# Batch loads into packed 192-byte rows, and weights staged in tiles of their own

## The chip, the cores and the metric

The kernel runs on one core of one Trainium2 chip. The metric is the device time of one execution in microseconds, lower is better; where there are several runs, their median.

## The reference

A gated linear attention runs over 4 batches, 8 heads, 768 steps and a head size of 48. Its output, laid side by side over the heads (3072 rows of 384), goes through a feed-forward layer that takes the larger of two projections:

```python
f = 1.0 / (1.0 + np.exp(-f_logit))
for t in range(S):
    state = f[:, :, t, :, None] * state + np.einsum('bhd,bhe->bhde', k[:, :, t], v[:, :, t])
    y[:, :, t] = np.einsum('bhd,bhde->bhe', q[:, :, t], state)

x = y.transpose(0, 2, 1, 3).reshape(B * S, H * D)
out = np.maximum(x @ w1, x @ w2) @ w_out      # w1, w2: 384 x 1024, w_out: 1024 x 384
```

All inputs and the output are float32.

## The kernel before

The 768 steps of a batch are cut into 6 chunks (`nch`) of 128 (`C`), which makes 24 chunks (`T`), numbered over the batches. In SBUF the partition is the step within the chunk.

**Loads.** For each of f, k, q and v there are two buffers (`lb`), used by even and odd batches: 128 partitions by 8 heads, 6 chunks and 64 floats (`DP`), of which 48 (`D`) are used. So every row of 48 floats, 192 bytes, begins on a multiple of 256 bytes. `load(i)` (L60) brings one chunk of all four inputs, 192 KB each; `load_batch(b, names)` (L67) brings all six chunks of a batch at once, 1.18 MB for each input. In DRAM the steps of a head lie one behind the other, so two rows that lie side by side in a partition are 128 steps apart in DRAM, and two rows in neighbouring partitions are adjacent there. All loads and all stores are issued on one queue, SyncE's (SP), in the order of the program text.

**Order of the queue.** Chunks 0 to 2, the weights w2 and w_out, chunk 3, the weight w1, chunks 4 and 5 (L81 to L88); then batch 1 (issued at the end of the loop's step 0), f and v of batch 2 (step 1), k and q of batch 2 (step 2), the stores of group 0 (steps 6 and 7), f and v of batch 3 (step 7), k and q of batch 3 (step 8), and the other stores. A store waits on the queue for its data, and all that is behind it waits too.

**Weights.** The three weight matrices have no tiles of their own: `w1_f`, `w2_f` and `wo_f` (L77 to L79) are views of the second buffers of f, k and q. They are read by `u_w2_cast` (VectorE), `u_wo_cast` (ScalarE) and `u_wd` (VectorE, `wd` = w1 - w2). The layer is computed as relu(x (w1 - w2)) w_out + x (w2 w_out), where w2 w_out is made once (`u_w2T`, `u_w2o`).

**The loop.** Each step i runs parts of several chunks: `s_y(i)` (state and output), `s_tr(i+2)` (transposes), `s_a(i+1)` (products within a chunk, masked), `s_cum(i+3)` (running sums of the gates, and scaled k and q on GpSimd), `s_xT(i)` (transpose of the result), `s_ell(i+4)` (the gate's logarithm, and v cast to bf16 on VectorE). Four chunks make a group. When a group is complete, `push_group` puts 16 units of the feed-forward layer into a list: eight `u_d` (a block of d_ff, the relu into `gT`) and two halves of `u_o` for each of four output tiles; the second half copies the result to `ob` (VectorE, L186) and stores it (L188). Between the parts of a step one unit each is taken from the list, four in a step, so a group's output copies fall into two steps out of four, two copies in each. Every engine works through its instructions in this order. The group's last units run after the loop.

The work tiles that the change touches have these numbers of buffers before: `gT` 2, `ob` 3, `e` 2, `tmp` 2, `xT` 3.

Of the kernel before, what the change touches and what calls it, by code (L numbers as in the profile page):

```python
# [11 lines left out]
F32 = mybir.dt.float32  # L12
BF16 = mybir.dt.bfloat16
# [4 lines left out]
def kernel(  # L18
# [15 lines left out]
    B, H, S, D = q.shape  # L34
    C = 128
    nch = S // C
    dm = H * D
    d_ff = moe_w1.shape[1]
    JG = dm // C
    FG = d_ff // C  # L40
    DP = 64
    NP = H // 2
    T = nch * B
    GT = B * C

    ctx.enter_context(tc.manual_schedule())
    consts = ctx.enter_context(tc.tile_pool(name="consts", bufs=1))
    work = ctx.enter_context(tc.tile_pool(name="work", bufs=2))
# [6 lines left out]

    SRC = (("f", f_logit), ("k", k), ("q", q), ("v", v))

    lb = {n: [consts.tile([C, H, nch, DP], F32, name=f"{n}b{x}") for x in range(2)] for n, _ in SRC}

    def load(i):  # L60
        b, c = divmod(i, nch)
# [11 lines left out]
    def loaded(i, name):  # L73
        b, c = divmod(i, nch)
        return lb[name][b % 2][:, :, c, 0:D]

    w1_f = lb["f"][1].rearrange("p h c d -> p (h c d)").rearrange("p (j f) -> p j f", j=JG)  # L77
    w2_f = lb["k"][1].rearrange("p h c d -> p (h c d)").rearrange("p (j f) -> p j f", j=JG)
    wo_f = lb["q"][1].rearrange("p h c d -> p (h c d)").rearrange("p (j f) -> p j f", j=FG)  # L79

    for i in range(3):  # L81
        load(i)
# [74 lines left out]
    xT_g = {}  # L157

    def push_group(g):
        gT = work.tile([C, FG, GT], BF16, name="gT", tag="gT")  # L160
        xT = xT_g[g]

        def u_d(f):
            ps = ps_m.tile([C, GT], F32, name="d", tag="mm")
            for j in range(JG):
                nc.tensor.matmul(out=ps, lhsT=wd[:, j, f * C:(f + 1) * C], rhs=xT[:, j, :],  # L166
                                 start=(j == 0), stop=(j == JG - 1))
            nc.scalar.activation(gT[:, f, :], ps, AF.Relu)  # L168

        hold = {}  # L170

        def u_o(b, half):
            ts = slice(b * C, (b + 1) * C)
            if half == 0:
                hold[b] = ps_m.tile([C, dm], F32, name="o", tag="mm")
            ps = hold[b]
            mms = [(xT[:, j, ts], w2o[:, j, :]) for j in range(JG)]
            mms += [(gT[:, f, ts], wo[:, f, :]) for f in range(FG)]
            cut = 6
            todo = range(0, cut) if half == 0 else range(cut, len(mms))  # L180
            for n in todo:
                nc.tensor.matmul(out=ps, lhsT=mms[n][0], rhs=mms[n][1],  # L182
                                 start=(n == 0), stop=(n == len(mms) - 1))
            if half == 1:
                ob = work.tile([C, dm], F32, name="ob", tag="ob", bufs=3)
                nc.vector.tensor_copy(ob, ps)  # L186
                r0 = (g * B + b) * C
                nc.sync.dma_start(out=out[r0:r0 + C, :], in_=ob)  # L188

        for f in range(FG):  # L190
            units.append(lambda f=f: u_d(f))
        for b in range(B):
            units.append(lambda b=b: u_o(b, 0))
            units.append(lambda b=b: u_o(b, 1))
# [9 lines left out]
    def s_ell(i):  # L204
        b, c = divmod(i, nch)
        t = {n: loaded(i, n) for n in "fkqv"}
        e = work.tile([C, dm], F32, name="e", tag="e")
        ell = ell_b[i % 2]
        nc.scalar.activation(e.rearrange("p (h d) -> p h d", h=H), t["f"], AF.Exp, scale=-1.0)  # L209
        nc.scalar.activation(ell[:, :, 0:D], e.rearrange("p (h d) -> p h d", h=H), AF.Ln, bias=1.0)  # L210
        vb = work.tile([C, dm], BF16, name="vb", tag="vb", bufs=6)
        nc.vector.tensor_copy(vb.rearrange("p (h d) -> p h d", h=H), t["v"])  # L212
        st[i] = {"ell": ell, "v": vb}
# [50 lines left out]
    def s_y(i):  # L264
        b, c = divmod(i, nch)
        s = st[i]
        am, vb, tr = s["am"], s["v"], s["tr"]
        old, new = st_b[b][c % 2], st_b[b][(c + 1) % 2]
        if c < nch - 1:
            sa = ps_s.tile([C, NP, 2 * D], F32, name="sa", tag="s")  # L270
            for p in range(NP):
                nc.tensor.matmul(out=sa[:, p, :],  # L272
                                 lhsT=s["kp"][:, 2 * p:2 * p + 2, :].rearrange("p h d -> p (h d)"),
                                 rhs=vb[:, 2 * p * D:(2 * p + 2) * D], start=True, stop=True)
            tmp = work.tile([C, NP, 2 * D], F32, name="tmp", tag="tmp")
            nc.vector.tensor_add(tmp, sa, old)  # L276
            for o in range(2):
                r, e = slice(o * DP, (o + 1) * DP), slice(o * D, (o + 1) * D)
                nc.gpsimd.tensor_mul(new[r, :, e], tmp[r, :, e],  # L279
                                     s["fl"][r, :].unsqueeze(2).to_broadcast([DP, NP, D]))  # L280
        y = ps_s.tile([C, dm], F32, name="y", tag="s")
        for p in range(NP):
            if c > 0:
                nc.tensor.matmul(out=y[:, 2 * p * D:(2 * p + 2) * D], lhsT=tr[:, 1, p, :],  # L284
                                 rhs=old[:, p, :], start=True, stop=False)
            for o in range(2):
                h = 2 * p + o
                ds = slice(h * D, (h + 1) * D)
                nc.tensor.matmul(out=y[:, ds], lhsT=am[:, o, p, :], rhs=vb[:, ds],  # L289
                                 start=(c == 0), stop=(c == 0 or o == 1))  # L290
        x = work.tile([C, dm], BF16, name="x", tag="x")
        nc.scalar.copy(x, y)  # L292
        s["x"] = x

    def s_xT(i):
        b, c = divmod(i, nch)
        s = st.pop(i)
        g, n = divmod(i, B)
        if n == 0:
            xT_g[g] = work.tile([C, JG, GT], BF16, name="xT", tag="xT", bufs=3)  # L300
        ps = ps_s.tile([C, JG, C], BF16, name="xtp", tag="s")
        for j in range(JG):
            nc.tensor.transpose(out=ps[:, j, :], in_=s["x"][:, j * C:(j + 1) * C], identity=ident)
        nc.vector.tensor_copy(xT_g[g][:, :, n * C:(n + 1) * C], ps)  # L304


    for i in range(-4, T):
        if i >= 0:
            s_y(i)
        unit()  # L310
        if 0 <= i + 2 < T:
            s_tr(i + 2)
        unit()
        if 0 <= i + 1 < T:
            s_a(i + 1)
        unit()
        if 0 <= i + 3 < T:
            s_cum(i + 3)
        unit()
        if i >= 0:  # L320
            s_xT(i)
        if i < B:
            unit()
            unit()
        if i >= 0 and i % B == B - 1:
            push_group(i // B)
        if 0 <= i + 4 < T:
            s_ell(i + 4)
        if i == 0:
            load_batch(1, "fkqv")  # L330
        if i >= 0 and i % nch == 1 and i // nch + 2 < B:
            load_batch(i // nch + 2, "fv")
        if i >= 0 and i % nch == 2 and i // nch + 2 < B:
            load_batch(i // nch + 2, "kq")
# [32 lines left out]
```

## Time and profile before

| | |
|---|---|
| median of 2 runs | 221.16 us (220.6 and 221.72) |
| the profiled execution's own time | 222.57 us |
| its span, first to last instruction | 220.8 us |
| busy: PE / VectorE / ScalarE / GpSimd | 145.7 / 101.4 / 86.5 / 75.5 us |
| mean granted TensorE clock | 0.876 |
| DMA | 28.54 MB, 129 GB/s on average |

The profile gives the busy time of each engine and cuts the span into 40 equal slices of 5.5 us; a digit there is a tenth of the slice. "PEclk" is the granted clock of TensorE in tenths. In rows of waits stand the engine and its line, what it waited for, the total in us, the number of times and the longest. Rows of a timeline begin with the start and the duration in us, then the engine, the line, the operation, what it writes and reads, and in brackets the idle time ahead of it and what ended it. "SPq" is the DMA queue of SyncE; a duration there is the time that issuing took, not the transfer. Rows of windows give, for a stretch of time, the busy time of each engine, the granted clock, the DMA engines' share and GB/s. L64 is line 64 of the kernel.

### The profile page before, as it was taken

Reading aid. Unit: us, or ns where it says so; the run is one execution under the profiler, and the core shown is the slowest. Engines: PE = TensorE matmul, PEld = TensorE weight load, DVE = VectorE, ACT = ScalarE, POOL = GpSimd, SP = SyncE. Lnnn points to the kernel's source line nnn. Section 1 sums busy time; section 2 is a strip of 40 time slices with the busy share of each in tenths; the row PEclk is TensorE's granted clock in tenths of the full one; section 3 lists DMA queues with packets and bytes.
Section 4 is the critical chain, followed back from the end, with each engine's and each line's share of the span. In section 5 each row is a group of like instructions: output and inputs, shape, how many; then the busy total and the mean of one; then the engine's idle time right before and its main releaser. Section 6 shows DMA issues by size and latency. Waiting matters only on the chain.

```text
span 220.8 us, 3530 instructions
## 1 busy us (share of the span) xinstructions
PE 145.7 (66%) x1384; PEld 87.6 (40%) x1384; DVE 101.4 (46%) x161; ACT 86.5 (39%) x200; POOL 75.5 (34%) x107
## 2 busy tenths in 40 slices
PE   0000169468700088995699970689998999999893
PEld 0000155345500044563345640345654565456451
DVE  8002333787200165762456540466665666564122
ACT  2000463644520027644176440176457645640610
POOL 8000035376300073553145430155553555520000
PEclk9999999955555569999589995599999999999999
DMA  8999999979999999999599989200210012002012
GB/s 123 163 172 393 256 324 173 107 133 163 163 168 163 163 163 166 163 166 179 150 159 167 167 150 186 100 0 0 74 71 3 0 73 76 0 3 106 36 39 107
DMA packets 48897, 28.54 MB, mean 129 GB/s; under 512 B 25584, under 2 KB 48112, under 8 KB 48880
## 3 DMA queue, kind: packets, MB, share of 16 engines
q1 hardware_dynamic: 48880, 28.32, 71.0%
q8 instruction: 11, 0.18, 0.4%
q14 instruction: 6, 0.05, 0.1%
HBM read 23.59 MB, written 4.72 MB: 128 GB/s over the span
## 4 chain that ended last, share of the span: by engine, by line
PE 33%; issue 19%; DMA 17%; POOL 14%; SPq 10%; ACT 4%; DVE 2%; POOLq 0%; DVEq 0%; ACTq 0%
PE o L182 12%; PE d L166 11%; SPq L70 10%; DMA out_dram<-ob 9%; DMA vb<-in_v_dram 8%; POOL qp L234 6%; POOL kp L233 5%; PE tr L242 4%; PE a L257 3%; ACT ei L229 3%; POOL st L108 1%; ACT gT L168 1%; PE y L284 1%; DVE ob L186 1%; PE y L289 1%
## 5 line engine op out<-in xcount | busy, mean ns | idle before, releaser
L233 POOL TENSOR_TENSOR kp<-kb,ei 128x384 bf16<-128x384 f32 x24 | 24.9, 1039 | 84.7 <-ACT ei L229 76.4
L166 PE MATMUL d<-xT,wd 128*128 128x512 bf16 x144 | 41.6, 410 | 14.1 <-DVE xT L304 13.9
L168 ACT ACTIVATE gT<-d 128x512 bf16<-128x512 f32 x48 | 29.0, 603 | 35.5 <-PE d L166 35.1
L182 PE MATMUL o<-wo,gT 128*128 128x384 bf16 x192 | 37.7, 326 | 0.0
L279 POOL TENSOR_TENSOR st<-tmp,fl 64x192 bf16<-64x192 f32 x40 | 20.1, 503 | 36.4 <-DVE tmp L276 35.0
L260 DVE TENSOR_TENSOR am<-a,mask 128x1024 bf16<-128x1024 f32 x24 | 29.2, 1219 | 4.3 <-PE a L257 4.3
L186 DVE COPY ob<-o 128x384 f32<-128x384 f32 x24 | 13.4, 558 | 35.7 <-PE o L182 20.5
L246 DVE COPY trs<-tr 128x1024 bf16<-128x1024 bf16 x24 | 16.6, 691 | 28.7 <-PE tr L242 28.7
L234 POOL TENSOR_TENSOR qp<-qb,ed 128x384 bf16<-128x384 f32 x24 | 27.1, 1129 | 0.0
L229 ACT ACTIVATE ei<-cum 128x384 f32<-128x384 f32 x24 | 11.7, 489 | 38.0 <-PE cum L223 38.0
L212 DVE CAST vb<-vb 128x384 bf16<-128x384 f32 x24 | 15.8, 658 | 19.5 <-DMA vb<-in_v_dram 19.5
L166 PEld LDWEIGHTS <-wd 128*128 128x128 bf16 x144 | 12.4, 102 | 24.2 <-issue 16.4
L182 PEld LDWEIGHTS <-gT 128*128 128x128 bf16 x192 | 17.8, 97 | 10.4
L292 ACT CAST x<-y 128x384 bf16<-128x384 f32 x24 | 11.2, 467 | 22.2 <-PE y L289 22.1
L134 PE MATMUL w2tp<-ident,w_h 128*128 128x128 bf16 x24 | 3.5, 308 | 22.3 <-DVE w_h L122 22.3
L272 PE MATMUL sa<-vb,kp 128*128 128x96 bf16 x80 | 7.3, 220 | 16.3 <-DVE tmp L276 15.5
L182 PE MATMUL o<-w2o,xT 128*128 128x384 bf16 x72 | 15.7, 326 | 0.0
L242 PE MATMUL tr<-ident,qp 128*128 128x128 bf16 x96 | 11.3, 251 | 6.2 <-POOL qp L234 5.6
L289 PE MATMUL y<-vb,am 128*128 128x48 bf16 x192 | 12.3, 191 | 2.2 <-DVE am L260 1.7
L221 PE MATMUL cum<-ell,ut 128*128 128x384 bf16 x24 | 9.1, 378 | 6.0 <-ACT ell L210 6.0
L209 ACT ACTIVATE e<-fb 128x384 f32<-128x384 f32 x24 | 13.0, 541 | 0.0
L210 ACT ACTIVATE ell<-e 128x384 bf16<-128x384 f32 x24 | 12.6, 523 | 0.9
(42 smaller groups left out, 183.7 us busy)
## 6 DMA issues: line engine op xcount, KB each, us to landing
out_dram<-ob SPq DMA_DIRECT2D x24, 192.0 KB, 1.9
kb<-in_moe_w_dram SPq DMA_DIRECT2D x1, 1536.0 KB, 7.8
qb<-in_moe_w_out_dram SPq DMA_DIRECT2D x1, 1536.0 KB, 11.0
fb<-in_moe_w_dram SPq DMA_DIRECT2D x1, 1536.0 KB, 7.9
fb<-in_f_logit_dram SPq DMA_DIRECT2D x6, 192.0 KB, 5.3
kb<-in_k_dram SPq DMA_DIRECT2D x6, 192.0 KB, 5.4
qb<-in_q_dram SPq DMA_DIRECT2D x6, 192.0 KB, 5.4
vb<-in_v_dram SPq DMA_DIRECT2D x6, 192.0 KB, 5.0
```

Of the source, the lines that this page charges most:

```text
L70: nc.sync.dma_start(out=lb[name][b % 2][:, :, :, 0:D].rearrange("p h c d -> p (h c) d"), in_=src[b].rearrange("h (c p) d -> p (h c) d", c= ...
L166: nc.tensor.matmul(out=ps, lhsT=wd[:, j, f * C:(f + 1) * C], rhs=xT[:, j, :], start=(j == 0), stop=(j == JG - 1))
L168: nc.scalar.activation(gT[:, f, :], ps, AF.Relu)
L182: nc.tensor.matmul(out=ps, lhsT=mms[n][0], rhs=mms[n][1], start=(n == 0), stop=(n == len(mms) - 1))
L212: nc.vector.tensor_copy(vb.rearrange("p (h d) -> p h d", h=H), t["v"])
L229: nc.scalar.activation(ei, ps[:, 0:dm], AF.Exp)
L233: nc.gpsimd.tensor_mul(kp[:, :, 0:D], t["k"], ei.rearrange("p (h d) -> p h d", h=H))
L234: nc.gpsimd.tensor_mul(qp[:, :, 0:D], t["q"], ed.rearrange("p (h d) -> p h d", h=H))
L242: nc.tensor.transpose(out=ps[:, n, p, :], in_=src[:, 2 * p:2 * p + 2, :].rearrange("p h d -> p (h d)"), identity=ident)
L246: nc.vector.tensor_copy(tr, ps)
L260: nc.vector.tensor_mul(am.rearrange("p o n c -> p (o n) c"), ps.rearrange("p o n c -> p (o n) c"), mask)
L279: nc.gpsimd.tensor_mul(new[r, :, e], tmp[r, :, e], s["fl"][r, :].unsqueeze(2).to_broadcast([DP, NP, D]))
```

## The change

The load buffers get rows of 48 floats instead of 64: a partition's 48 rows of a batch then adjoin, and a row begins at a multiple of 192 bytes. The buffers shrink from 12288 to 9216 bytes a partition, and no longer have the size of a weight matrix; the three weights get tiles of their own, 12288 bytes a partition each. Five kinds of work tiles get fewer buffers. The text of `load`, `load_batch` and `loaded` stays as it is, and so do the order of the queue and of the loop.

```diff
-    lb = {n: [consts.tile([C, H, nch, DP], F32, name=f"{n}b{x}") for x in range(2)] for n, _ in SRC}
+    lb = {n: [consts.tile([C, H, nch, D], F32, name=f"{n}b{x}") for x in range(2)] for n, _ in SRC}
...
-    w1_f = lb["f"][1].rearrange("p h c d -> p (h c d)").rearrange("p (j f) -> p j f", j=JG)
-    w2_f = lb["k"][1].rearrange("p h c d -> p (h c d)").rearrange("p (j f) -> p j f", j=JG)
-    wo_f = lb["q"][1].rearrange("p h c d -> p (h c d)").rearrange("p (j f) -> p j f", j=FG)
+    w1_f = consts.tile([C, JG, d_ff], F32, name="w1_f")
+    w2_f = consts.tile([C, JG, d_ff], F32, name="w2_f")
+    wo_f = consts.tile([C, FG, dm], F32, name="wo_f")
...
-        gT = work.tile([C, FG, GT], BF16, name="gT", tag="gT")
+        gT = work.tile([C, FG, GT], BF16, name="gT", tag="gT", bufs=1)
...
-                ob = work.tile([C, dm], F32, name="ob", tag="ob", bufs=3)
+                ob = work.tile([C, dm], F32, name="ob", tag="ob", bufs=2)
...
-        e = work.tile([C, dm], F32, name="e", tag="e")
+        e = work.tile([C, dm], F32, name="e", tag="e", bufs=1)
...
-            tmp = work.tile([C, NP, 2 * D], F32, name="tmp", tag="tmp")
+            tmp = work.tile([C, NP, 2 * D], F32, name="tmp", tag="tmp", bufs=1)
...
-            xT_g[g] = work.tile([C, JG, GT], BF16, name="xT", tag="xT", bufs=3)
+            xT_g[g] = work.tile([C, JG, GT], BF16, name="xT", tag="xT", bufs=2)
```

## The prediction

> **What bounds the kernel now.** I read the page's slices first, then the table of waits, then the DMA queue's own timeline, then VectorE's timeline around the long waits. The slices are 5.5 us each.
>
> ```profile
> span 220.8 us, 3530 instructions
> PE   0000169468700088995699970689998999999893
> PEclk9999999955555569999589995599999999999999
> DMA  8999999979999999999599989200210012002012
> GB/s 123 163 172 393 256 324 173 107 133 163 163 168 163 163 163 166 163 166 179 150 159 167 167 150 186 100 0 0 74 71 3 0 73 76 0 3 106 36 39 107
> ```
>
> The DMA engines are nearly always busy up to 138 us, at about 165 GB/s, and nearly idle afterwards. PE has two holes in that time (near 65 us and 135 us) and is dense after it. So up to 138 us the loads set the pace, and after it the engines do. The waits and the queue say which loads:
>
> ```profile
> ACT wo L126 <- DMA qb<-in_moe_w_out_dram: 23.3, 1, 23.3
> DVE vb L212 <- DMA vb<-in_v_dram: 19.5, 1, 19.5
> DVE ob L186 <- DMA out_dram<-ob: 14.3, 2, 9.5
> SPq L70 <- DVE wd L129: 4.6, 1, 4.6
> ```
> ```profile
> 38.30 1.14 SPq L64 DMA_DIRECT2D vb<-in_v_dram  x1
> 44.20 0.82 SPq L70 DMA_DIRECT2D fb<-in_f_logit_dram  x1
> 59.26 7.27 SPq L70 DMA_DIRECT2D vb<-in_v_dram  x1
> 88.06 6.55 SPq L70 DMA_DIRECT2D qb<-in_q_dram  x1
> 94.72 11.90 SPq L188 DMA_DIRECT2D out_dram<-ob  x4
> 106.84 0.71 SPq L70 DMA_DIRECT2D fb<-in_f_logit_dram  x1
> 121.77 7.80 SPq L70 DMA_DIRECT2D qb<-in_q_dram  x1
> ```
> ```profile
> 76.31 0.36 DVE L212 CAST vb<-vb 128x384 bf16<-128x384 f32 x1 [19.53 <-DMA vb<-in_v_dram]
> 95.91 0.56 DVE L186 COPY ob<-o 128x384 f32<-128x384 f32 x1 [0.80 <-PE o L182]
> 99.16 0.56 DVE L186 COPY ob<-o 128x384 f32<-128x384 f32 x1
> 99.63 1.22 DVE L260 TENSOR_TENSOR am<-a,mask 128x1024 bf16<-128x1024 f32 x1
> 105.70 0.56 DVE L186 COPY ob<-o 128x384 f32<-128x384 f32 x1 [4.86 <-DMA out_dram<-ob]
> 127.76 0.56 DVE L186 COPY ob<-o 128x384 f32<-128x384 f32 x1
> 138.91 0.56 DVE L186 COPY ob<-o 128x384 f32<-128x384 f32 x1 [9.45 <-DMA out_dram<-ob]
> ```
>
> ScalarE waits 23.3 us for w_out, which stands in the queue behind the first twelve chunk loads. VectorE waits until 76.3 us for v of batch 1, the fourth of its batch loads. Then, twice, the fourth output copy of a group waits for a buffer: its store was queued behind k and q of the next batch, lands when they have drained (105.6 and 138.8 us), and VectorE stands still until then. After 138.9 us no load is left. So four things in a row set the end: the chunk loads, the three batches of loads, the two held copies, and 82 us of engine work.
>
> **What a loaded row costs.** A chunk load moves 192-byte rows. For a batch load the page's packet counts tell more:
>
> ```profile
> DMA packets 48897, 28.54 MB, mean 129 GB/s; under 512 B 25584, under 2 KB 48112, under 8 KB 48880
> ```
> ```profile
> 30.00:32.00 2.00, 1.18 (x11) 0.65 (x8) 1.35 (x4) 1.17 (x4) 1.94 (x2) 1.00 1.03 414
> 34.00:36.00 2.00, 2.00 (x7) 0.91 (x6) 1.26 (x2) 0.62 (x3) 1.75 (x1) 1.00 1.53 163
> 42.00:43.00 1.00, 0.08 (x3) 0.08 (x4) 1.00 (x2) 0.97 (x4) 0.96 (x2) 1.00 0.32 32
> 43.00:44.00 1.00, 0.52 (x12) 0.35 (x12) 1.00 (x1) 0.81 (x2) 1.00 (x2) 1.00 0.00 0
> 44.00:45.00 1.00, 0.00 (x0) 0.00 (x0) 1.00 (x2) 0.00 (x0) 0.97 (x1) 0.57 0.07 16
> 45.00:46.00 1.00, 0.97 (x12) 0.69 (x12) 0.98 (x3) 0.00 (x0) 0.20 (x1) 0.50 0.11 31
> 46.00:76.30 30.30, 11.97 (x132) 8.49 (x129) 8.60 (x13) 8.81 (x23) 8.84 (x12) 0.50 1.04 167
> 76.30:103.50 27.20, 22.95 (x236) 13.92 (x236) 16.80 (x26) 13.67 (x33) 14.17 (x18) 0.90 1.08 166
> 103.50:108.30 4.80, 1.72 (x8) 0.89 (x8) 1.55 (x4) 0.25 (x1) 0.89 (x2) 0.72 0.39 143
> 108.30:138.00 29.70, 21.48 (x215) 12.55 (x213) 12.95 (x19) 12.94 (x32) 10.25 (x13) 0.84 1.02 168
> ```
>
> (The last two columns of the windows are the DMA share and GB/s.) Between 512 bytes and 2 KB lie 48112 - 25584 = 22528 packets. 3072 of them are rows of the 24 stores and 1024 rows of w_out, both 1536 bytes. The 18432 left are 1536 for each of the twelve batch loads of 1.18 MB: 768 bytes, four rows, each. So a batch load reads four rows at a time; a chunk load reads them singly (24 x 1024 = 24576 of the 25584 small packets). Yet both run alike: 192 x 16 / 163 = 18.8 ns for a row on one of 16 engines in a chunk load, 192 x 16 / 167 = 18.4 ns in a batch load. Reading four times as wide buys nothing, so I take it that the price sits where the row is written, in SBUF. Long rows are far cheaper by the byte: at 414 GB/s, when w1's 4 KB rows move, a byte costs 16 / 414 = 0.0386 ns.
>
> **The change part by part.**
>
> *Weights in their own tiles.* f of batch 1 no longer waits for wd (4.6 us above); with nothing earlier in the second set of buffers, its load is issued behind the last chunk load, near 39.5 us instead of 44.2. What counts is not the 4.6 us but the hole in the transfers: the DMA shares from 42 to 46 us are 0.32, 0.00, 0.07 and 0.11, so 4 - 0.5 = 3.5 us of it are idle. All that hangs on batch 1 and 2 comes 3.5 us earlier: **-3.5 us**. Nothing else is late there: k, q and v of batch 1 follow on the queue, and no wait of theirs stands in the table.
>
> *ob with two buffers.* Now the third copy of a group, not the fourth, needs the buffer of the first, whose store is stuck. So VectorE is held at the copy of 99.16, shifted to 95.7, until 102.1 (105.6 - 3.5). What was done before the wait then comes after it: that copy and the mask product (99.16 to 99.63, and 1.22 us), about 1.7 us, and PE's y behind the product, so 1.8 us. The fourth store and f of batch 3 behind it on the queue leave that much later, and the hole from 103.5 to 108.3 grows by as much. The same happens at 127.76. **+1.8 twice, +3.6 us**. Bounds: nothing, if the loads drain before the copy; 2.5 us each if the whole distance between two copies (95.91 - 93.4) is lost.
>
> ```profile
> L186 DVE COPY ob<-o x24: 556/558/559, 93.4 to 217.4; 128x384 f32<-128x384 f32 x24
> DMA to landing us min/median/max: 1.8/1.9/10.9
> 215.66 0.56 DVE L186 COPY ob<-o 128x384 f32<-128x384 f32 x1 [1.23 <-PE o L182]
> 217.44 0.56 DVE L186 COPY ob<-o 128x384 f32<-128x384 f32 x1 [1.23 <-PE o L182]
> ```
>
> In the tail copies come 1.78 us apart, so a buffer is wanted 3.56 us after its copy began; 0.56 + 1.9 us suffice, and it costs nothing.
>
> *gT and e with one buffer, xT with two, tmp with one.* Nothing. gT and xT are read by PE alone, and PE is past the old readers before the matmul or transpose whose result overwrites them. e is written and read by ScalarE. tmp is read by POOL's product into the state, which VectorE's next addition reads anyway. At a change of batch, where it reads another state, a chunk without an addition lies between.
>
> *The engines' reads of packed rows.* The same 48-element runs at another stride:
>
> ```profile
> L209 ACT ACTIVATE e<-fb 128x384 f32<-128x384 f32 x24 | 13.0, 541 | 0.0
> L210 ACT ACTIVATE ell<-e 128x384 bf16<-128x384 f32 x24 | 12.6, 523 | 0.9
> ```
>
> A strided source costs 541 ns beside 523 for a contiguous one; the change keeps runs of 48, so I take nothing.
>
> *Packed destinations.* This decides. Before, each 192-byte row starts on a multiple of 256 bytes; after, it starts at a multiple of 192, in chunk loads too. Taken modulo 256 the starts are 0, 192, 128 and 64 in turn, and of four rows two cross a 256-byte line, as 64 + 128 and 128 + 64 bytes. No row of the trace shows a write across such a line. From below: in a batch load all rows of a partition now adjoin, so they could be written as one long run; at the weights' 0.0386 ns a row would take 7.4 ns, a gain of 60%. From above: a crossing row costs as two, 50% more. In between I take the nearest thing that has a price: the crossing row pays a second time for its shorter piece, 64 bytes at 0.0386 = 2.5 ns, on half of the rows 1.24 ns of 18.6, **6.6%**. It falls on all rows that the path waits for: 4.72 MB of chunk loads at 163 GB/s, 29 us, and the three batches, 30.3 + 27.2 + 29.7 us, together 116 us: **+7.7 us**.
>
> Against this, the chunk loads read rows from HBM that start at the same four places, and at 18.8 ns they are no slower than batch loads whose 768-byte reads start on the line. That speaks for a price of nothing, but reads there may be covered by the writes.
>
> The Trainium skill, "DMA: Bandwidth & Descriptors", section "How a descriptor splits into AXI transactions", says of reads that a descriptor off a 256-byte boundary begins at the boundary below, in beats of 32 bytes. By that, a row from 0, 64, 128 and 192 takes 6, 8, 10 and 12 beats, on average 9 for 6, as an estimate 96 bytes more a row. The trace does not show it for reads (18.8 against 18.4 ns), and has no such write.
>
> *Sum.* The profiled run took 222.57 us, 1.8 around its span of 220.8. 222.57 - 3.5 + 3.6 + 7.7 = 230.4. The two runs have a median of 221.16, 1.41 lower; on that scale **229.0 us**, 3.5% slower.
>
> **The rivals.**
>
> 1. *The line costs nothing*: 222.57 - 3.5 + 3.6 = 222.7, or 221.3 us against the median. For it: reads across the line are free. Against: writes are what seems to bound a row.
>
> 2. *The row pays in full*: a row pays from the line below its start, so for 0, 192, 128 or 64 bytes more, on average 96, which at 0.0386 is 3.7 ns or 20% of 116 us: +23, so 244 us; with a crossing row as two, +58, so 279 us. (This is the page's rule carried over from reads to writes.) For it: a row of 18.6 ns is far more than the 7.4 ns of its bytes, so something is paid per write. Against: a cost that is fixed per row may cover the extra piece.
>
> 3. *Adjoining rows are written together*, on the other side. Only batch loads gain. At the weights' byte cost a batch takes 4.72 MB / 414 = 11.4 us instead of 28, so all three long waits go: 19.5 + 4.9 + 9.45 = 33.8 us, 187 us against the median. It decides once a batch load takes some 5% less (7.2 to 6.8 us): 87 us x 5% = 4.4 us, 2%. For it: the destination of a partition is one run of 9216 bytes, and long rows run at 414 GB/s. Against: the source stays in pieces of 192 or 768 bytes, and a write as long as the partition's run would need reads from 48 places.
>
> **How the numbers follow.** Two per cent (216.7 to 225.6 us) is about what can be told from no change. Forecast, a price of 3 to 12% (225.6 to 236 us): 0.34. Rival 1: 0.31. Rival 2, above 236 us: 0.17. Rival 3: 0.18, a third of it for a small gain that ends above 212 us. Slower is 0.34 + 0.17 = 0.51, same 0.31, faster 0.18. The range 212 to 246 us leaves out 0.12 of rival 3 and 0.08 of rival 2; the forecast's own is 225.6 to 236.
>
> **What would show it.** Batch 1's f load issued near 39.5 us and no hole at 43 us: the first step. VectorE waiting for a store at the third copy of groups 0 and 1: the second. Batch loads 7.7 us apart instead of 7.2, windows at 155 GB/s instead of 167, and v of batch 1 landing near 77 us: the third. At 167 GB/s the third step is wrong, at 140 too small, above 180 of the wrong sign. Packets of 192 bytes in batch loads would say that reads are no longer four rows wide. If the loads no longer end before the engines do, or if VectorE waits for something other than v and the stores, the chain is wrong.

## The result, and the profile after

The changed kernel takes 201.62 us (200.52 and 202.73), the kernel before 221.16: a ratio of 0.912, with a 95% interval from 0.888 to 0.935. It is faster, where a loss of 3.5% was forecast, and it lies 10 us below the range. Executions of a kernel that lie over 1.5% above its fastest one are counted as slow, and all ratios here compare the others.

The page of the changed kernel, its slices (here of 5.0 us) and packet counts:

```profile
span 198.7 us, 3510 instructions
PE   0000249757761989999899149999989999998993
PEclk9999999955555699999999756999999999999998
DMA  6999999999997899928997920002200111012022
GB/s 125 198 215 374 289 300 261 207 207 211 220 223 176 201 219 205 253 87 193 210 216 160 248 89 3 0 9 75 79 3 2 59 63 40 3 41 110 9 80 81
DMA packets 48897, 28.54 MB, mean 144 GB/s; under 512 B 25584, under 2 KB 48112, under 8 KB 48880
```

The engines' work is nearly the same (PE 142.6 us busy for 145.7; VectorE, ScalarE and GpSimd within 0.3 us), and the packet counts are the same to the last one: batch loads still read four rows at a time, chunk loads one. But where the kernel before moved 163 to 168 GB/s, this one moves 204 to 220 in the windows shown below, and the loads are over near 115 us instead of 138.

The queue's timeline, from the last chunk load to the loads of batch 3, and VectorE's rows at the same places as before:

```profile
35.23 0.83 SPq L64 DMA_DIRECT2D vb<-in_v_dram  x1
36.28 0.83 SPq L70 DMA_DIRECT2D fb<-in_f_logit_dram  x1
49.10 4.94 SPq L70 DMA_DIRECT2D vb<-in_v_dram  x1
66.65 4.90 SPq L70 DMA_DIRECT2D kb<-in_k_dram  x1
72.01 5.21 SPq L70 DMA_DIRECT2D qb<-in_q_dram  x1
79.87 8.56 SPq L188 DMA_DIRECT2D out_dram<-ob  x4
88.65 0.71 SPq L70 DMA_DIRECT2D fb<-in_f_logit_dram  x1
100.77 6.19 SPq L70 DMA_DIRECT2D qb<-in_q_dram  x1
```
```profile
61.94 0.36 DVE L212 CAST vb<-vb 128x384 bf16<-128x384 f32 x1 [7.63 <-DMA vb<-in_v_dram]
85.10 0.56 DVE L186 COPY ob<-o 128x384 f32<-128x384 f32 x1 [0.19 <-PE o L182]
114.77 0.56 DVE L186 COPY ob<-o 128x384 f32<-128x384 f32 x1 [7.57 <-DMA out_dram<-ob]
116.38 0.55 DVE L186 COPY ob<-o 128x384 f32<-128x384 f32 x1
```

Batch 1's first load follows the last chunk load at once. v of batch 1 lands at 61.9 us instead of 76.3. The third copy of group 0 waits for no store, because k and q of batch 2 had drained by then. Group 1 is still held, now at its third copy, until 114.8. Its fourth copy comes at 116.38 instead of 138.91, 22.5 us earlier, and from there to the end of the span both kernels need the same: 198.7 - 116.4 = 82.3 us, and 220.8 - 138.9 = 81.9. So in these two profiled runs the whole gain was made while loads ran.

The windows say how: two stretches of batch loads and one of chunk loads of the changed kernel (the last two columns are DMA share and GB/s).

```profile
38.00:62.00 24.00, 14.46 (x161) 10.22 (x161) 14.16 (x20) 11.61 (x30) 11.96 (x14) 0.55 0.91 204
62.00:78.00 16.00, 12.71 (x120) 7.34 (x121) 10.43 (x16) 9.10 (x21) 8.20 (x11) 0.82 0.98 215
33.00:36.00 3.00, 3.00 (x19) 1.69 (x17) 0.95 (x1) 1.10 (x4) 2.76 (x2) 1.00 1.19 220
```

A chunk load's row took 18.8 ns and now takes 192 x 16 / 220 = 14.0 ns; a batch load's took 18.4 and now 192 x 16 / 215 = 14.3 ns. Chunk loads gain as much as batch loads, though their rows do not adjoin: in a chunk load neighbouring rows of a partition lie 6 x 192 = 1152 bytes apart. So for chunk loads the prediction's third rival, adjoining rows written as one, is out already, and so is wider reading for all loads. What suggests itself is where each row lies.

### The profile page after: what moved, and what is told of

It is laid out like the page before. It is cut to its first block, busy times and chain, and to the rows that moved or that the text cites. A ratio compares the mean times of both kernels' runs of the same rounds, so it can differ in the third digit from the quotient of the medians.

```text
span 198.7 us, 3510 instructions
## 1 busy us (share of the span) xinstructions
PE 142.6 (72%) x1373; PEld 86.9 (44%) x1384; DVE 101.1 (51%) x161; ACT 86.5 (44%) x200; POOL 75.5 (38%) x107
## 4 chain that ended last, share of the span: by engine, by line
PE 40%; SPq 24%; POOL 12%; DMA 10%; issue 5%; ACT 5%; DVE 3%; POOLq 0%; ACTq 0%; DVEq 0%
PE o L182 17%; SPq L64 16%; PE d L166 12%; DMA vb<-in_v_dram 6%; SPq L70 6%; POOL qp L234 6%; POOL kp L233 6%; PE tr L242 5%; DMA out_dram<-ob 4%; ACT ei L229 3%; PE a L257 3%; ACT gT L168 1%; PE y L284 1%; DVE ob L186 1%; PE y L289 1%
## 5 line engine op out<-in xcount | busy, mean ns | idle before, releaser
L166 PE MATMUL d<-xT,wd 128*128 128x512 bf16 x133 | 38.7, 399 | 2.2 <-DVE xT L304 1.0
L279 POOL TENSOR_TENSOR st<-tmp,fl 64x192 bf16<-64x192 f32 x40 | 20.1, 501 | 18.6 <-DVE tmp L276 17.1
L289 PEld LDWEIGHTS <-am 128*128 128x128 bf16 x192 | 10.8, 103 | 9.8 <-DVE am L260 9.1
L284 PE MATMUL y<-st,trs 128*128 128x96 bf16 x80 | 10.9, 215 | 2.9 <-ACT fl L231 2.2
```

The costliest lines, as they stand in the source:

```text
L279: nc.gpsimd.tensor_mul(new[r, :, e], tmp[r, :, e], s["fl"][r, :].unsqueeze(2).to_broadcast([DP, NP, D]))
```

## Experiments

### Was it the rows or the weights?

The first kernel keeps packed rows, but lets the weights share the second buffers again, with the old numbers of work buffers. Four packed buffers are as large as three weights:

```diff
+    second = consts.tile([C, 4 * H * nch * D], F32, name="second")
+    lb = {n: [consts.tile([C, H, nch, D], F32, name=f"{n}b0"),
+              second[:, x * H * nch * D:(x + 1) * H * nch * D].rearrange("p (h c d) -> p h c d", h=H, c=nch)]
+          for x, (n, _) in enumerate(SRC)}
...
+    w1_f = second[:, 0 * JG * d_ff:1 * JG * d_ff].rearrange("p (j f) -> p j f", j=JG)
...
```

> Packed rows, but the weights again share the second buffers of f, k and q, and the work tiles have their old numbers of buffers. If the rows made the gain: the hole before batch 1 is back (about +4 us against the changed kernel) and the early hold at the third copy is gone (-1.7 us), so about 203 us. If the weights' own tiles made it: near 221 us.

It took 205.12 us (4 runs), 0.926 of the kernel before (0.920 to 0.932). Measured beside it, the kernel before took 221.99, so packed rows alone are worth 16.9 us. The hole before batch 1 is there again; the queue's last chunk load and first batch load:

```profile
37.01 0.70 SPq L67 DMA_DIRECT2D vb<-in_v_dram  x1
43.27 0.83 SPq L73 DMA_DIRECT2D second<-in_f_logit_dram  x1
```

The second kernel does the opposite: the kernel before with two weights in tiles of their own and the changed numbers of work buffers, but padded rows. The third weight, w_out, stays in the second buffer of q.

```diff
-    w1_f = lb["f"][1].rearrange("p h c d -> p (h c d)").rearrange("p (j f) -> p j f", j=JG)
-    w2_f = lb["k"][1].rearrange("p h c d -> p (h c d)").rearrange("p (j f) -> p j f", j=JG)
+    w1_f = consts.tile([C, JG, d_ff], F32, name="w1_f")
+    w2_f = consts.tile([C, JG, d_ff], F32, name="w2_f")
...
```

> Padded rows as before, but w1 and w2 in tiles of their own and the smaller numbers of buffers of the change. If the rows made the gain: the prediction's sum without its last term, 222.7 us for a profiled run and about 221 us in the median; VectorE held at the third copies of groups 0 and 1. If the weights' own tiles made it: near 202 us.

It took 222.56 us (10 runs), a ratio of 1.004 (1.000 to 1.007). VectorE's rows in it:

```profile
73.35 0.36 DVE L212 CAST vb<-vb 128x384 bf16<-128x384 f32 x1 [16.58 <-DMA vb<-in_v_dram]
102.08 0.56 DVE L186 COPY ob<-o 128x384 f32<-128x384 f32 x1 [4.69 <-DMA out_dram<-ob]
103.69 0.55 DVE L186 COPY ob<-o 128x384 f32<-128x384 f32 x1
136.95 0.56 DVE L186 COPY ob<-o 128x384 f32<-128x384 f32 x1 [12.28 <-DMA out_dram<-ob]
138.56 0.55 DVE L186 COPY ob<-o 128x384 f32<-128x384 f32 x1
```

v of batch 1 is 3.0 us earlier than before (73.35 for 76.31), both groups are held at the third copy, and the fourth copy of group 1 comes at 138.56 instead of 138.91: what the hole gives, the two holds take back. So without packed rows there is no gain, and packed rows alone make most of it.

### What two buffers of ob cost

```diff
-                ob = work.tile([C, dm], F32, name="ob", tag="ob", bufs=2)
+                ob = work.tile([C, dm], F32, name="ob", tag="ob", bufs=3)
```

> The changed kernel with three buffers of ob. If the hold costs what the prediction says (1.8 us for each held group, and only group 1 is held in the changed kernel): about 199.9 us, with the wait moved from the third copy to the fourth. If it costs nothing because the wait ends at the same time: 201.6 us.

The changed kernel with three buffers took 199.54 us, 0.899 of before (0.894 to 0.905), 2.1 us less than the changed kernel's median, and the wait moved to the fourth copy:

```profile
115.66 0.56 DVE L186 COPY ob<-o 128x384 f32<-128x384 f32 x1 [7.28 <-DMA out_dram<-ob]
```

The two kernels' intervals overlap, so the size is rough. With packed rows and shared weights (205.12, also three buffers of `ob`) as the other side, the weights' own tiles are worth about 5.6 us; `gT`, `e`, `tmp` and `xT` differ between these two as well. That is more than with padded rows, because the chunk loads end earlier while the first load of batch 1 still waits for `wd`: with packed rows and shared weights it was issued at 43.27, hardly earlier than before (44.20), and the DMA shares from 39 to 45 us were 0.78, 0.02, 0.00, 0.00, 0.08 and 0.04, so some 5 us were idle instead of 3.5.

### Which rows are dear?

A kernel that only loads went through pitches and starts of the rows. Its output is not the layer's; it computes nothing.

```diff
+            d = big[:, x * W + off:x * W + off + N * pitch].rearrange("p (n e) -> p n e", e=pitch)[:, :, 0:D]
+            nc.sync.dma_start(out=d, in_=(q, k_, v, f_logit)[x][x].rearrange("h (c p) d -> p (h c) d", c=nch))
...
```

> A kernel of loads alone, with no arithmetic: fifteen sets of four batch loads, the sets one after the other, each into rows of another pitch (in floats: 64, 48, 64 begun 64, 128 and 192 bytes later, 52, 56, 60, 72, 80, 96, 112, 128, 64, 48); then ten sets of eight chunk loads with pitches 384, 288, 64, 48, 96, 128, 320, 336, 384, 288. A padded set of four batch loads should take about 29 us and a packed one 22 us, from the two traces. Theory A (what costs is that all rows start at the same place modulo 256 bytes): pitches 64 and 128 are slow wherever they begin, 384 in chunk loads too; 52, 56, 60, 72, 80, 112 are as fast as 48; 96, with two places, lies between. Theory B (a start on the 256-byte line itself costs): 64 begun 64, 128 or 192 bytes later is fast, 22 us. Theory C (a dense destination is what is cheap, by the bytes spanned): time rises steadily from 48 to 128, and 52 and 56 lie near 48. Theory D (only rows that adjoin are cheap, written as one run): 48 alone is fast and 52 already takes 29 us; chunk loads of pitch 288 are as slow as 384.

Windows within the sets of pitch 64, 48, 64 begun 64, 128 and 192 bytes later, 52, and 128:

```profile
core 0: us, POOL busy (x), PEclk, DMA share, GB/s
6.00:28.00 22.00, 0.00 (x0) 1.00 1.10 163
34.00:50.00 16.00, 0.00 (x0) 1.00 1.04 217
56.00:78.00 22.00, 0.00 (x0) 1.00 1.11 163
84.00:97.00 13.00, 0.00 (x0) 1.00 0.89 248
102.00:116.00 14.00, 0.00 (x0) 1.00 0.87 247
124.00:138.00 14.00, 0.00 (x0) 1.00 1.08 194
296.00:322.00 26.00, 0.00 (x0) 1.00 1.10 163
```

None of the four theories fits. Rows of one and the same pitch run at 163 or at about 250 GB/s, depending on where they begin: that is against A, C and D. B has 64 bytes later wrong, which is as slow as the tile's own start. But B and the prediction counted from the tile's start. In the compiled program the first buffer lies at byte 16512 of each partition; 16512 = 64 x 256 + 128. (No trace shows this address, but these sets say the same: the fast rows are those that begin 128 or 192 bytes after the tile.) So "64 begun 0 and 64 bytes later" begin 128 and 192 bytes past a multiple of 256, and their rows of 192 bytes lie *across* a 256-byte line. "128 later" begins on a line, and "192 later" begins at 64 and ends on one. **By this count the padded rows of the kernel before all lie across a line; of packed rows, half do.**

All other sets fit. Pitch 128 (always 128 past) is slow; 52 and 60, with 11 of 16 rows across, ran at 194 GB/s, 56 and 72, with 5 of 8, at 201, and 80, 96 and 112, with half, at 216 to 218. In the sets of chunk loads, pitches 384, 64, 128 and 320, whose rows all begin 128 past a line, ran at 163 to 164, and 288, 48, 96 and 336, with half across, at 204 to 224. Padded rows off the line (248) are also faster than packed ones (217), though they do not adjoin.

### The same, counted from address 0

A second kernel of loads took start, length and pitch apart, with each set waited for.

> A kernel of loads alone (the buffer is first set to zero): 25 sets of four batch loads of 1.18 MB, each set ended by a small copy on VectorE that the next set waits for. A set is given by the row's length, its pitch (both in floats) and the byte modulo 256 at which its rows start, counted from the partition's address 0, which takes in that the compiled program puts the first buffer at byte 16512, 128 past a multiple of 256. Theory L (a row that lies across a 256-byte line costs more than one inside it): rows of 48 floats that start at 0, 32 or 64 take about 4.5 us a load (267 GB/s), those that start at 80, 96, 112, 128, 160, 192 or 224 about 7.2 us (163 GB/s), packed ones about 5.5. Rows of 32 floats: slow at 160 and 192, fast at 0 and 128. Rows of 16: slow at 224 alone. Rows of 64: slow at 128. Theory P (what is slow is a piece whose length is not a power of two): 48 floats at 0, 32 and 64 are slow, 128 and 192 (64 and 128 bytes) fast. Theory H (it is the start in the upper half of a line that is slow): 80, 96 and 112 are fast, and 32 floats at 128 are slow.

VectorE's copies that end the sets; in brackets its wait for the set's four loads. In order: 48 floats at 128 (the buffer had been set to zero before it), 0, 32, 64, 80, 224, packed; 32 floats at 128 and 160; 16 floats at 0 and 224; 64 floats at 0 and 128.

```profile
51.44 0.29 DVE L49 COPY scr<-big 128x256 f32<-128x256 f32 x1 [31.25 <-DMA big<-in_f_logit_dram]
72.32 0.29 DVE L49 COPY scr<-big 128x256 f32<-128x256 f32 x1 [20.58 <-DMA big<-in_f_logit_dram]
93.00 0.29 DVE L49 COPY scr<-big 128x256 f32<-128x256 f32 x1 [20.39 <-DMA big<-in_f_logit_dram]
113.88 0.29 DVE L49 COPY scr<-big 128x256 f32<-128x256 f32 x1 [20.59 <-DMA big<-in_f_logit_dram]
145.24 0.29 DVE L49 COPY scr<-big 128x256 f32<-128x256 f32 x1 [31.07 <-DMA big<-in_f_logit_dram]
...
302.71 0.29 DVE L49 COPY scr<-big 128x256 f32<-128x256 f32 x1 [31.37 <-DMA big<-in_f_logit_dram]
327.57 0.29 DVE L49 COPY scr<-big 128x256 f32<-128x256 f32 x1 [24.56 <-DMA big<-in_f_logit_dram]
...
379.44 0.29 DVE L49 COPY scr<-big 128x256 f32<-128x256 f32 x1 [25.74 <-DMA big<-in_f_logit_dram]
425.15 0.30 DVE L49 COPY scr<-big 128x256 f32<-128x256 f32 x1 [45.42 <-DMA big<-in_f_logit_dram]
...
516.61 0.29 DVE L49 COPY scr<-big 128x256 f32<-128x256 f32 x1 [45.41 <-DMA big<-in_f_logit_dram]
605.72 0.29 DVE L49 COPY scr<-big 128x256 f32<-128x256 f32 x1 [88.81 <-DMA big<-in_f_logit_dram]
624.43 0.29 DVE L49 COPY scr<-big 128x256 f32<-128x256 f32 x1 [18.42 <-DMA big<-in_f_logit_dram]
648.60 0.29 DVE L49 COPY scr<-big 128x256 f32<-128x256 f32 x1 [23.87 <-DMA big<-in_f_logit_dram]
```

Theory L holds in every set, those not shown here included; the first two sets, run again at the end, gave 31.23 and 21.00 us. A row of 48 floats inside a line costs the same from 0, 32 and 64; 16 bytes further, from 80 on, every start costs 31 us. The reads are the same for all rows of one length, so it is the place in SBUF that counts. Rows of 32 floats are cheap at 128 and dear at 160: so it is the line, not the upper half (H). Rows of 48 at 0 are cheap though 192 is no power of two (P). Four loads have 4 x 6144 / 16 = 1536 rows on an engine, so crossing costs (31.2 - 20.5) / 1536 = 7.0 ns a row. For rows of 64 bytes, of which an engine has 4608, the whole set nearly doubles, from 45.4 to 88.8 us: there a crossing row costs as two. So the price is no constant: 9.4 ns for a row of 64 bytes, 7.0 for 192, and for 256, which a set moves in 1152 rows on an engine, (23.87 - 18.42) / 1152 = 4.7.

### The line in the kernel itself

If that is so, the kernel before needs no packing, only 128 bytes:

```diff
-    lb = {n: [consts.tile([C, H, nch, DP], F32, name=f"{n}b{x}") for x in range(2)] for n, _ in SRC}
+    SH = 32
+    raw = {n: [consts.tile([C, H * nch * DP + 64], F32, name=f"{n}b{x}") for x in range(2)] for n, _ in SRC}
+    lb = {n: [t[:, SH:SH + H * nch * DP].rearrange("p (h c d) -> p h c d", h=H, c=nch) for t in raw[n]] for n, _ in SRC}
```

> The kernel before, with all load buffers moved by 128 bytes and 256 bytes longer, nothing else. By theory L every padded row then lies inside a 256-byte line and a batch load takes about 4.6 us instead of 7.2: v of batch 1 lands near 64 us instead of 76.3, no copy of group 0 is held, and of group 1 a copy for some 2 to 4 us: about 196 us, below the changed kernel. By theory P or H, and if only the packing counts, it stays at 221 us.

Four runs took 193.44, 195.54, 198.78 and 199.27 us, and the ratio to the kernel before is 0.876 (0.867 to 0.885): below the changed kernel, by 128 bytes alone. The weights, as views of these buffers, move along. The profiled run (199.27) has v of batch 1, the held copy of group 1, and two windows of batch loads:

```profile
63.76 0.36 DVE L214 CAST vb<-vb 128x384 bf16<-128x384 f32 x1 [9.31 <-DMA vb<-in_v_dram]
115.62 0.56 DVE L188 COPY ob<-o 128x384 f32<-128x384 f32 x1 [3.56 <-DMA out_dram<-ob]
60.00:72.00 12.00, 6.12 (x40) 3.27 (x41) 5.34 (x9) 1.67 (x3) 4.04 (x6) 0.50 0.87 247
97.00:107.00 10.00, 9.36 (x96) 5.54 (x95) 6.53 (x10) 5.91 (x15) 4.96 (x8) 1.00 0.91 260
```

v of batch 1, the hold and the rate are as theory L had them. The same three lines, with `D` for `DP`, were then put into the changed kernel, with its packed rows:

> The changed kernel with its load buffers moved by 128 bytes and 256 bytes longer. Theory L: of packed rows two in four lie across a line wherever the first one starts, so nothing changes: 201.6 us. If moving the buffers, or their length, is what helped the padded kernel: some 8 us less.

202.11 us, a ratio of 0.911 (0.903 to 0.920), the same as without. So neither the shift nor the longer tile helps by itself; it helps the kernel whose rows it takes off the line. Last, padded rows off the line together with tiles of their own for w1 and w2, three buffers of `ob`, five of `vb`, and the other work tiles as in the changed kernel:

> Padded rows moved by 128 bytes, w1 and w2 in tiles of their own, three buffers of ob, one of gT, e and tmp, two of xT, five of vb. By theory L the shifted loads, no hole before batch 1, and hardly a held copy: about 191 us, below all others. If the engines already set the pace with packed rows: 199 us, as with three buffers of ob.

Five runs took 187.22 to 193.81 us, with a median of 187.5 and a ratio of 0.844 (0.838 to 0.850): the fastest of all, 14 us below the changed kernel's median.

## Why the prediction was wrong

**What bounds the kernel: right.** The loads set the pace up to the held copy of group 1, and the 82 us behind it did not change.

**Weights in their own tiles, -3.5 us, and ob with two buffers, +3.6 us: right for padded rows, as a sum.** With padded rows the two together gave a ratio of 1.004 (1.000 to 1.007), where the sum without its last term, 221.3 us, gives 1.001. v of batch 1 came 3.0 us earlier, and both third copies were held. With packed rows group 0 is not held, since its loads drain earlier; the prediction's lower bound of nothing then applies to that one. Three buffers instead of two gave about 2.1 us where 1.8 were put on one hold. And the weights' own tiles were worth about 5.6 us there instead of 3.5, since faster chunk loads leave a longer hole; so with packed rows the two terms came to about -3.5 together, not to +0.1.

**gT, e, tmp and xT, and the strided reads: not tried one by one,** but the padded kernel that has the four smaller numbers of buffers agrees with the sum. In the changed kernel, ScalarE's exponential of the strided f takes 542 ns where it took 541, as forecast.

**Packed destinations, +7.7 us: wrong, and this is nearly the whole miss.** The step that failed is the sentence "Before, each 192-byte row starts on a multiple of 256 bytes". The description of the kernel before says the same. That is so counted from the tile, but the tile begins 128 bytes past such a multiple. Nor is it true that no row of the trace crosses such a line: by the start found above, all rows of the chunk and batch loads before do. So the change did not bring half of the rows onto a line; it took half of them off it. The mechanism that was named, a row across a 256-byte line paying for a second piece, was the right one, with the sign turned round, and its price was too small as well: 7.0 ns a crossing, not 2.5. With the right start and price the term is -0.5 x 7.0 / 18.6 = -19% of 116 us, or -22 us. Measured, packed rows alone gave -16.9 (205.12 against 221.99), and on top of the other parts -20.9 (201.62 against 222.56). The prediction's own sign for this, a rate above 180 GB/s, is what the windows show (204 and 215).

**The argument from reads.** Chunk loads read HBM rows across lines at no visible price, and that was held to speak for a price of nothing. The caution behind it, that writes may cover the reads, was right. But all 192-byte rows of the trace before were written across a line, so the trace had no cheap row to compare with. The 18.6 ns that looked like the price of a row were the price of a crossing row; one inside a line costs (20.5 us / 1536 rows) 13.3 ns at most, with the latency of the set in it.

**The rivals.** The gain fell on the side of the third rival, but not by its mechanism, so it does not speak for it: chunk loads gain the same without adjoining rows, and padded rows off the line are faster than packed ones. The first rival's price of nothing is out. The second's dearest case, a crossing row as two, holds for rows of 64 bytes; a row of 192 bytes pays about half as much again.

## What to carry to other kernels

Where short rows are loaded, count their place from the address that the program gives the buffer, not from the start of the tile; a row that fits into a 256-byte line was cheaper here wherever it lay within one. Before a price is set on moving something across a boundary, make sure on which side it lies now: a trace in which all rows are alike cannot say whether they are all cheap or all dear. And a transfer rate far from that of long rows is worth one kernel of loads alone, since 128 bytes of shift gave more here than the whole change.

## What the hardware showed that was not expected

A loaded row of 192 bytes costs the same wherever it starts inside a 256-byte line of the partition (20.58, 20.39 and 20.59 us for starts at 0, 32 and 64), and across the line about 50% more; one of 64 bytes costs 96% more. The rule of the Trainium skill on reads ("DMA: Bandwidth & Descriptors", "How a descriptor splits into AXI transactions") lets a start off the boundary pay for the bytes before it; for these writes the three sets from 0, 32 and 64 show no such price, only that of the line.

Left open: why a packed set, half of whose rows cross, is better than the mean of the two kinds (24.56 us for (20.5 + 31.2) / 2 = 25.9), and what of the price is paid in the DMA engine and what in SBUF.
